# Two tokens to a partition in w's first loads, u spread by a product, W_out rows four to a partition

## The chip, the cores and the metric

The kernel runs on one core of one Trainium2 chip. The metric is the device time in microseconds, the median over several runs. A core has TensorE (PE, the matrix unit), VectorE (DVE), ScalarE (ACT), GpSimd (POOL) and SyncE (SP, which here only issues DMAs). All share an on-chip memory of 128 partitions; PE writes into PSUM.

## The reference

Two parts follow each other: a recurrent attention with a decay (B=4, H=8, S=768, D=48), and a two-layer MLP with a leaky ReLU on its 3072 output tokens (384 to 2048 to 384). All inputs and the output are float32.

```python
for t in range(S):
    kt, vt, rt, wt = k[:, :, t], v[:, :, t], r[:, :, t], w[:, :, t]
    cur = np.einsum('bhd,bhe->bhde', u[None] * kt, vt)
    y[:, :, t] = np.einsum('bhd,bhde->bhe', rt, state + cur)
    state = wt[:, :, :, None] * state + np.einsum('bhd,bhe->bhde', kt, vt)
x = y.transpose(0, 2, 1, 3).reshape(B * S, H * D)
h = x @ w_in
out = np.maximum(0.01 * h, h) @ w_out
```

## The kernel before, in words

**Attention.** The 3072 tokens are cut into 24 chunks of 128, six to a batch. A chunk has its 128 tokens on the partitions. Its w, r, k and v come in four loads (`load_in`, L190) of 192 KB, each 1024 runs of 192 bytes: one run per token and head. The steps of chunk i are named in the code, and the prediction uses these names:

- `log` (`a_log`, L229, ACT): the logarithm of w, as `lw`.
- `cum` (`a_cum`, L234 and L236, PE): the running sum of `lw` over the tokens, as a product with a triangle `tri`, and four one-column products with `ones` that give the chunk's whole sums for the decay of the state.
- `neg`: the negative sum that includes the token itself. In the first four chunks (`EARLY`) it is a second product with a triangle `trin` (`a_cum2`, L243, PE), later a DVE operation (`a_neg`, L247).
- `exp` and `exn` (L254, L257, ACT): exponentials of both sums. `kr` (L261, DVE): they are multiplied onto k and r.
- `trans` and `rkT` (L293, PE, then a copy L298 on ACT or L300 on DVE): the transpose of `kr`, eight blocks through the tile `trp`; for the later chunks (`BY_DMA`) one transposing DMA instead (L304, issued by SP).
- `scores` (L314, tile `at`), `m0` and `m1` (L322, DVE: the causal mask), `mix` (L333, L339, tile `y`), `ysb` (L347, DVE: adds the term of u).
- The term of u: `t1` (L265, r times `ukb`, POOL), `t2` (L269, times k, POOL), `diag` (L280, sum over D, DVE), `vsc` (L284, times v, POOL). `ukb` is u on all 128 partitions, loaded by SP (L193).
- The state: `kv` (L352, PE), `tt` (L360, or a copy), `st` (L370, POOL).
- `ytr` and `xT` (L380, PE, then a copy L388 on ACT): y transposed into `xT`, which the MLP reads; for the last chunks (`Y_BY_DMA`) a transposing DMA (L383).

**MLP.** W_in and W_out come in four quarters of 768 KB each (L200, L207) into float32 buffers, and DVE casts each to bfloat16 (L214, L217). The tokens are taken in blocks of 128 or 256 (`sizes`). For a block, `hid` (L409, tile `hp`) makes the 2048 hidden values in 16 groups of 128 columns of W_in, three matmuls for each; `act` (L415, ACT) applies the leaky ReLU into `gt`; `out` (L421, tile `op`) makes 128 tokens of output with 16 matmuls, in four parts that each need one quarter of W_out; `copy` (L428) and `issue` (L432) on ACT store them.

**Order.** The order of all instructions is written by the kernel itself before it emits anything. The class `Order` holds every step with its engine, a cost, the steps that it needs and the PSUM buffers it takes. It picks again and again the step that can begin earliest by these costs, and the instructions are emitted in that order, so each engine's list is fixed. Steps of rank 100 and above (the MLP) fill PE between those of the attention. Loads go out in the order of the list `queue`, all on SP's queue:

```python
queue = [('in', 0), ('u', 0), ('in', 1), ('in', 2), ('w_in', 0), ('in', 3), ('w_in', 1), ('w_in', 2), ('w_in', 3), ('in', 4), ('w_out', 0), ('w_out', 1), ('w_out', 2), ('w_out', 3)] + [("in", i) for i in range(5, NCH)]
```

Ahead of PE's first steps, up to a planned time of `WARM`, gaps are filled with dummy products of 512 columns (`scratch`, L548). The constants `tri`, `trin` and the identity are made on POOL, `ones`, the operand of the dummies and the zeroed padding on DVE. PSUM's eight buffers are given out as one for `cum`, one for `trp`, three for the rest of the attention (`att`) and three for the MLP (`mlp`, which also serves `neg` of the first chunks).

Of the kernel before, what the change touches and what calls it, by code (L numbers as in the profile page):

```python
# [8 lines left out]
F32 = mybir.dt.float32  # L9
# [6 lines left out]
class Order:  # L16
# [20 lines left out]
    def run(self, pools):  # L37
# [3 lines left out]
        taken = {p: [] for p in pools}  # L41
# [9 lines left out]
        def ready(name):  # L51
            t = 0.0
            for n in self.steps[name][6]:
                n = self.real(n)
                if n not in ends:
                    return None
                same = self.steps[n][0] == self.steps[name][0] != "DMA"
                t = max(t, ends[n] - (self.steps[n][4] if same else 0.0))
            want = {}
            for pool, _ in self.steps[name][7]:  # L60
                want[pool] = want.get(pool, 0) + 1
            for pool, n in want.items():
                old = len(taken[pool]) + n - 1 - pools[pool]
                for x in range(max(0, old - n + 1), old + 1):
                    until = self.real(taken[pool][x])
                    if until not in ends:
                        return None
                    t = max(t, ends[until])
            return t

        while any(todo.values()):
# [23 lines left out]
            ends[item[2]] = t + took + lag  # L95
            for pool, until in takes:
                taken[pool].append((until, item[2][1]) if isinstance(until, str) else until)
# [7 lines left out]
def kernel(  # L105
# [11 lines left out]
    nc = tc.nc  # L117
# [18 lines left out]
    inpool = ctx.enter_context(tc.tile_pool(name="inpool", bufs=NIN))  # L136
    work = ctx.enter_context(tc.tile_pool(name="work", bufs=3))
    gpool = ctx.enter_context(tc.tile_pool(name="gpool", bufs=2))
    opool = ctx.enter_context(tc.tile_pool(name="opool", bufs=NOUTB))
    ps_cum = ctx.enter_context(tc.tile_pool(name="ps_cum", bufs=1, space=bass.MemoryType.PSUM))  # L140
    ps_tr = ctx.enter_context(tc.tile_pool(name="ps_tr", bufs=1, space=bass.MemoryType.PSUM))
    ps_att = ctx.enter_context(tc.tile_pool(name="ps_att", bufs=3, space=bass.MemoryType.PSUM))
# [3 lines left out]
    trin = const.tile([128, 128], BF16, name="trin")  # L146
# [4 lines left out]
    lw_b = [const.tile([128, H, 64], BF16, name=f"lw{i}") for i in range(NB3)]  # L151
    kr_b = [const.tile([128, 2 * H, 64], BF16, name=f"kr{i}") for i in range(NB3)]
# [6 lines left out]
    def constants():  # L159
        nc.gpsimd.memset(tri[:], 1.0)  # L160
# [4 lines left out]
        nc.gpsimd.memset(trin[:], -1.0)  # L165
        nc.gpsimd.affine_select(
            out=trin[:], in_=trin[:], compare_op=ALU.is_ge, fill=0.0, base=0,
            pattern=[[1, 128]], channel_multiplier=-1,
        )
# [3 lines left out]
        for t in lw_b + kr_b:  # L173
            nc.vector.memset(t[:, :, D:64], 0.0)
# [7 lines left out]
    def load_in(i, name):  # L182
        b, c = divmod(i, C)
        src = {"w": w, "r": r, "k": k, "v": v}[name]
        if not ins[i]:
# [6 lines left out]
    def load_u():  # L192
        nc.sync.dma_start(out=ukb[:], in_=u.rearrange("h d -> (h d)").partition_broadcast(128))  # L193
# [11 lines left out]
    def load_w_out(q):  # L205
# [3 lines left out]
            in_=moe_w_out[q * JQ * 128 : (q + 1) * JQ * 128, :].rearrange("(t p) n -> p t n", p=128),  # L209
# [20 lines left out]

    def a_cum(i):
        lw = lw_b[i % NB3]
        cum = att[i]["cum"] = ps_cum.tile([128, 512], F32, name="cum")
# [7 lines left out]
    def a_cum2(i):  # L241
        cum2 = att[i]["neg"] = ps_mlp.tile([128, H, D], F32, name="cum2", tag="mlp")
        nc.tensor.matmul(cum2[:], lhsT=trin[:], rhs=lw_b[i % NB3][:, :, 0:D], start=True, stop=True)  # L243
# [45 lines left out]
    def a_trans(i):  # L289
        trp = att[i]["trp"] = ps_tr.tile([128, 2, NP, 128], BF16, name="trp", tag="tr")  # L290
# [102 lines left out]
    sizes = [256, 256, 128, 128, 128, 128, 128, 128, 128, 128, 128, 128, 128, 128, 128, 256, 128, 256, 256]  # L393
# [7 lines left out]
    def m_hid(q, j, nj):  # L401
# [4 lines left out]
        for jj in range(nj):  # L406
            wq, f0 = divmod((j + jj) * 128, FQ)
            for t in range(KT):
                nc.tensor.matmul(  # L409
                    hp[:, jj, :], lhsT=w_in_b[:, wq, t, f0 : f0 + 128],  # L410
# [28 lines left out]
    BY_DMA = range(11, NCH)  # L439
    Y_BY_DMA = range(14, NCH)  # L440
    WARM = 18.0
    RCAST = -1
    SLACK = 1.2
    RACT = 12
# [3 lines left out]
    add("const", "POOL", 2.2, constants, rank=-1)  # L448
    users = []
    users = []  # L450
    users = []
    queue = [('in', 0), ('u', 0), ('in', 1), ('in', 2), ('w_in', 0), ('in', 3), ('w_in', 1), ('w_in', 2), ('w_in', 3), ('in', 4), ('w_out', 0), ('w_out', 1), ('w_out', 2), ('w_out', 3)] + [("in", i) for i in range(5, NCH)]
    for kind, n in queue:
        if kind == "u":
            add("u", "DMA", 0.55, load_u, lag=1.95)
            continue
        past_user = users[-NIN:][:1] if len(users) >= NIN else []
        if kind == "in":
            for x in ("w", "r", "k", "v"):
                add((x, n), "DMA", 1.07, load_in, n, x, lag=1.95, needs=past_user)  # L460
            users.append(("done", n))
        else:
            load, cast = (load_w_in, cast_w_in) if kind == "w_in" else (load_w_out, cast_w_out)
            add((kind, n), "DMA", 2.3, load, n, lag=1.95, needs=past_user)
            add(("cast", kind, n), "DVE", 0.97, cast, n, needs=[(kind, n)], rank=RCAST)
            users.append(("cast", kind, n))
    for i in range(NCH):
        c = i % C

        def step(name, eng, took, f, *needs, args=(), lag=0.06, takes=()):  # L470
            add((name, i), eng, took, f, i, *args, lag=lag, rank=-1 if eng == "DMA" else i, takes=takes,
# [6 lines left out]
        step("log", "ACT", 0.52, a_log, "w", *past(3, "cum"))  # L478
        step("cum", "PE", 0.27, a_cum, "log", *past(1, "exp", "neg"), lag=0.18)
        step("exp", "ACT", 0.49, a_exp, "cum", *past(3, "st", "kr"))  # L480
        if early:
            step("neg", "PE", 0.17, a_cum2, "log", "cum", lag=0.18, takes=(("mlp", "exn"),))
# [4 lines left out]
        step("t1", "POOL", 1.0, a_t1, "r", ("u",), *past(2, "t2"))  # L487
# [4 lines left out]
        if i in BY_DMA:  # L492
            step("rkT", "DMA", 1.6, a_rkT_dma, "kr", *past(3, "mix"), lag=2.2)
            order.alias(("trans", i), ("rkT", i))
        else:
            step("trans", "PE", 0.45, a_trans, "kr", *past(1, "rkT"), lag=0.3)
# [85 lines left out]
```

## Time and profile before

| | |
|---|---|
| median of 7 runs | 190.17 us (188.21 to 191.35) |
| the profiled execution | 188.21 us, with a span of 186.5 us |
| PE busy | 176.3 us, 95% of the span, 2138 matmuls |
| DVE, ACT, POOL busy | 113.6, 110.4 and 114.5 us |
| hid (L409) | 912 matmuls: 672 of 128 columns, 240 of 256 |
| out (L421) | 384 matmuls of 384 columns |
| DMA | 34.8 MB in 125063 packets, 187 GB/s in the mean |
| granted PE clock | 0.999 |

How to read the rows. In the page, a row of 40 digits cuts the span into 40 slices; each digit is the busy share in tenths. A row of a stage has, after its two ends, for PE, weight loads (PEld), DVE, ACT and POOL the busy microseconds and the number of instructions, and then the granted clock, the mean share of the 16 DMA engines and GB/s. A row of the timeline has the start in microseconds, the length, the engine ("SPq" is SP's queue of issued DMAs), the line, what is written and read, a count, and in brackets how long the engine stood idle before it and what released it. A row of a group has line, engine, operation, tiles and shapes with a count, then the busy time, the mean in ns, and the idle time before with what ended it. The recorded length of one matmul includes the way through the array, so matmuls overlap: their pace is read from the time that a series takes.

### The profile page before, as it was taken

What the parts mean: (1) busy time and instruction counts of PE and PEld (TensorE: products, weight loads), DVE (VectorE), ACT (ScalarE), POOL (GpSimd) and SP (SyncE); (2) the same over time, 40 slices, a digit from 0 to 9 for tenths busy, and PEclk for the clock granted to TensorE, in tenths of its full rate; (3) what the DMA queues carried; (4) which work ended last, traced back from release to release, by engine and by line L of the source; (5) the groups of instructions that cost most, each with busy time, mean ns of one, the idle gap of its engine ahead of it and who ended that gap; (6) DMA issues with size and microseconds to landing.
All of it is one profiled execution on the core that took longest, in us unless ns stands there. A gap on an engine that the chain in (4) does not pass through costs nothing.

```text
span 186.5 us, 5284 instructions
## 1 busy us (share of the span) xinstructions
PE 176.3 (95%) x2138; PEld 132.3 (71%) x2140; DVE 113.6 (61%) x184; ACT 110.4 (59%) x216; POOL 114.5 (61%) x142
## 2 busy tenths in 40 slices
PE   7999659899999999999999999999999999999993
PEld 2555547766777978797788788778867886787751
DVE  2277895584588799995796677453776574550000
ACT  3465747832756875684785576467456874364721
POOL 3299675604848999999788876653868488320000
PEclk9999999999999999999999999999999999999999
DMA  6999899799999989999899999699989999712012
GB/s 117 206 188 272 191 385 204 268 374 206 224 241 185 219 156 210 175 233 184 189 211 185 165 213 199 121 227 171 222 176 218 158 200 162 192 25 63 0 42 84
DMA packets 125063, 34.80 MB, mean 187 GB/s; under 512 B 118256, under 2 KB 123504, under 8 KB 125040
## 3 DMA queue, kind: packets, MB, share of 16 engines
q1 hardware_dynamic: 121584, 29.76, 84.3%
q10 hardware_dynamic: 3456, 4.72, 8.2%
q8 instruction: 16, 0.26, 0.6%
q14 instruction: 7, 0.06, 0.1%
HBM read 25.36 MB, written 4.72 MB: 161 GB/s over the span
## 4 chain that ended last, share of the span: by engine, by line
PE 68%; SPq 13%; DMA 13%; ACT 2%; issue 1%; POOL 1%; ACTq 0%; POOLq 0%
PE op L421 28%; PE hp L409 27%; SPq L190 11%; DMA in<-in_w_dram 9%; DMA in<-in_k_dram 4%; PE at L314 3%; PE cum L234 2%; PE y L339 2%; PE trp L293 1%; SPq L200 1%; PE y L333 1%; PE kv L352 1%; PE ytr L380 1%; ACT lw L229 1%; ACT osb L428 1%
## 5 line engine op out<-in xcount | busy, mean ns | idle before, releaser
L409 PE MATMUL hp<-xT,w_in_b 128*128 128x128 bf16 (+1 forms) x912 | 71.3, 233 | 1.0 <-DVE w_in_b L214 1.0
L421 PE MATMUL op<-w_out_b,gt 128*128 128x384 bf16 x384 | 69.6, 326 | 0.0
L409 PEld LDWEIGHTS <-w_in_b 128*128 128x128 bf16 x912 | 61.5, 98 | 6.8 <-DVE w_in_b L214 1.6
L415 ACT ACTIVATE gt<-hp 128x512 bf16<-128x512 f32 x96 | 55.3, 597 | 14.0 <-PE hp L409 11.2
L421 PEld LDWEIGHTS <-gt 128*128 128x128 bf16 x384 | 34.9, 98 | 20.2
L322 DVE TENSOR_TENSOR mt<-at,tri 128x512 bf16<-128x512 f32 x48 | 30.9, 682 | 12.0 <-PE at L314 9.1
L370 POOL TENSOR_TENSOR st<-tt,e 48x192 bf16<-48x192 f32 x40 | 25.2, 630 | 19.6 <-DVE tt L360 16.7
L261 DVE TENSOR_TENSOR kr<-e,in 128x768 bf16<-128x768 f32 x24 | 27.9, 1164 | 11.7 <-ACT e L257 6.2
L269 POOL TENSOR_TENSOR t<-t,in 128x384 f32<-128x384 f32 x24 | 28.7, 1194 | 9.2 <-DMA in<-in_k_dram 8.1
L265 POOL TENSOR_TENSOR t<-in,ukb 128x384 f32<-128x384 f32 x24 | 26.2, 1093 | 11.9 <-DMA in<-in_r_dram 5.9
L284 POOL TENSOR_TENSOR vsc<-in,diag 128x384 f32<-128x384 f32 x24 | 21.8, 909 | 8.1 <-DVE diag L280 5.7
L428 ACT COPY osb<-op 128x384 f32<-128x384 f32 x24 | 11.4, 477 | 23.5 <-PE op L421 23.4
L229 ACT ACTIVATE lw<-in 128x384 bf16<-128x384 f32 x24 | 12.5, 522 | 13.3 <-DMA in<-in_w_dram 12.9
L247 DVE SCALAR_TENSOR_TENSOR neg<-cum,lw 128x384 f32<-128x384 f32 x20 | 11.0, 551 | 14.0 <-ACT e L254 14.0
L347 DVE TENSOR_TENSOR ysb<-y,vsc 128x384 bf16<-128x384 f32 x24 | 13.3, 553 | 8.1 <-PE y L339 6.8
L254 ACT ACTIVATE e<-cum 128x388 f32<-128x388 f32 x24 | 11.9, 495 | 10.3 <-PE cum L236 3.7
L280 DVE TENSOR_REDUCE diag<-t 128x8 f32<-128x384 f32 x24 | 13.1, 544 | 3.7 <-POOL t L269 3.7
L548 PE MATMUL scratch<-idle 128*128 128x512 bf16 x44 | 13.0, 430 | 1.4 <-DVE idle L172 1.3
L257 ACT ACTIVATE e<-neg 128x384 f32<-128x384 f32 x20 | 10.5, 524 | 5.7 <-DVE neg L247 5.1
L276 POOL CAST vb<-in 128x384 bf16<-128x384 f32 x20 | 13.0, 649 | 0.9 <-DMA in<-in_v_dram 0.8
L314 PE MATMUL at<-rkT 48*128 48x128 bf16 x192 | 9.5, 219 | 1.9 <-ACT rkT L298 1.9
L314 PEld LDWEIGHTS <-rkT 48*128 48x128 bf16 x192 | 5.4, 94 | 6.1 <-ACT rkT L298 3.1
(43 smaller groups left out, 129.8 us busy)
## 6 DMA issues: line engine op xcount, KB each, us to landing
in<-in_w_dram SPq DMA_DIRECT2D x24, 192.0 KB, 4.6
in<-in_r_dram SPq DMA_DIRECT2D x24, 192.0 KB, 4.5
in<-in_k_dram SPq DMA_DIRECT2D x24, 192.0 KB, 4.7
in<-in_v_dram SPq DMA_DIRECT2D x24, 192.0 KB, 4.5
out_dram<-osb ACTq DMA_DIRECT2D x24, 192.0 KB, 3.5
ws<-in_moe_w_in_dram SPq DMA_DIRECT2D x4, 768.0 KB, 6.7
ws<-in_moe_w_out_dram SPq DMA_DIRECT2D x4, 768.0 KB, 7.3
rkT<-kr SPq DMA_TRANSPOSE x13, 4.3
```

The source lines that it names most:

```text
L190: nc.sync.dma_start(out=ins[i][name], in_=src[b, :, c * L : (c + 1) * L, :].rearrange("h p d -> p h d"))
L229: nc.scalar.activation(out=lw_b[i % NB3][:, :, 0:D], in_=ins[i]["w"], func=AF.Ln)
L261: nc.vector.tensor_tensor(out=kr_b[i % NB3][:, :, 0:D], in0=e, in1=ins[i]["kr"], op=ALU.mult)
L265: nc.gpsimd.tensor_tensor(out=t1[:], in0=flat(ins[i]["r"]), in1=ukb[:], op=ALU.mult)
L269: nc.gpsimd.tensor_tensor(out=flat(t2[:]), in0=att[i]["t1"][:], in1=flat(ins[i]["k"]), op=ALU.mult)
L284: nc.gpsimd.tensor_tensor(out=vsc[:], in0=ins[i]["v"], in1=att[i]["diag"][:].unsqueeze(2).to_broadcast([128, H, D]), op=ALU.mult,)
L314: nc.tensor.matmul(ats[x][:, p, :], lhsT=rkT[r0 : r0 + D, 0, p, :], rhs=rkT[r0 : r0 + D, 1, p, :], start=True, stop=True,)
L322: nc.vector.tensor_tensor(out=att[i]["mt"][:, x], in0=att[i]["ats"][x][:], in1=tri[:].unsqueeze(1).to_broadcast([128, NP, 128]), op=ALU.mult,)
L370: nc.gpsimd.tensor_tensor(out=sn[r0 : r0 + D, :, x * D : (x + 1) * D], in0=tt[r0 : r0 + D, :, x * D : (x + 1) * D], in1=el[r0 : r0 + D, :] ...
L409: nc.tensor.matmul(hp[:, jj, :], lhsT=w_in_b[:, wq, t, f0 : f0 + 128], rhs=xT[:, t, t0 : t0 + mb], start=(t == 0), stop=(t == KT - 1),)
L415: nc.scalar.activation(out=gts[q][:, j : j + nj, :], in_=hps.pop((q, j))[:], func=AF.Prelu, alpha=0.01)
L421: nc.tensor.matmul(ops[q, ts][:], lhsT=gts[q][:, j, ts * 128 : (ts + 1) * 128], rhs=w_out_b[:, j, :], start=(j == 0), stop=(j == NFT - 1),)
```

## The change

- The w of two neighbouring chunks (0 and 1, 2 and 3) is loaded by one DMA, `load_wp`: partition p holds tokens 2p and 2p+1 of the 256, a run of 384 bytes for each head. `a_logp` takes the logarithm of both chunks at once. Chunk 2m then lies on partitions 0 to 63 and chunk 2m+1 on 64 to 127, so `a_cum` and `a_cum2` of these chunks make each sum by two products over 64 partitions, for even and odd tokens, with triangles `tri2` and `trin2` that fit this order. The one buffer for w pairs makes the second load wait for the first logarithm.
- u is loaded as one row of 1536 bytes, issued by ACT; a product with a row of ones (`spread_u`, float32) puts it on 128 partitions in PSUM, and DVE copies it to `ukb`.
- A quarter of W_out is loaded with four neighbouring rows on each partition. So that `gt` fits, `m_hid` takes W_in's columns four apart.
- The `Order` gives PSUM buffers to whichever is free instead of in turn, `cum` and `trp` share one pool of five with `att`, several costs and ranks (`OFF`, `RCAST`, `RACT`) are others, `sizes` has nine blocks of 256 tokens where there were five, chunk 10's `rkT` is now made by DMA, and the y of chunks 14 to 17 is transposed on PE instead of by DMA. Before the first 6 us of plan a dummy is counted at 0.45 us.

```diff
     def load_u():
-        nc.sync.dma_start(out=ukb[:], in_=u.rearrange("h d -> (h d)").partition_broadcast(128))
+        nc.scalar.dma_start(out=u_row[:], in_=u.rearrange("h d -> (h d)").rearrange("(a n) -> a n", a=1))
+
+    def spread_u():
+        ub = stage["u"] = ps_att.tile([128, DM], F32, name="ub", tag="att")
+        nc.tensor.matmul(ub[:], lhsT=one_row[:], rhs=u_row[:], start=True, stop=True)
+
+    def copy_u():
+        nc.vector.tensor_copy(out=ukb[:], in_=stage["u"][:])
+
+    def load_wp(m):
+        t = ins[2 * m]["wp"] = wpool.tile([128, H, 2 * D], F32, name="wp")
+        b, c = divmod(2 * m, C)
+        nc.sync.dma_start(
+            out=t[:], in_=w[b, :, c * L : (c + 2) * L, :].rearrange("h (p j) d -> p h (j d)", j=2)
+        )
...
-            in_=moe_w_out[q * JQ * 128 : (q + 1) * JQ * 128, :].rearrange("(t p) n -> p t n", p=128),
+            in_=moe_w_out[q * JQ * 128 : (q + 1) * JQ * 128, :].rearrange("(p t) n -> p t n", p=128),
...
+    def a_logp(m):
+        t = ins[2 * m]["wp"]
+        nc.scalar.activation(
+            out=lwp_b[m][:, :, :, 0:D].rearrange("p j h d -> p h j d"),
+            in_=t.rearrange("p h (j d) -> p h j d", j=2), func=AF.Ln,
+        )
+
     def a_cum(i):
+        if i < EARLY:
+            r0, m = 64 * (i % 2), i // 2
+            cum = att[i]["cum"] = ps_att.tile([128, 512], F32, name="cum", tag="att")
+            for j in range(2):
+                nc.tensor.matmul(
+                    cum[:, 0:DM], lhsT=tri2[r0 : r0 + 64, j, 2 * r0 : 2 * r0 + 128],
+                    rhs=lwp_b[m][r0 : r0 + 64, j, :, 0:D], start=(j == 0), stop=False, skip_group_check=True,
+                )
+            for p in range(NP):
+                for j in range(2):
+                    nc.tensor.matmul(
+                        cum[:, DM + p : DM + p + 1], lhsT=pair(lwp_b[m][r0 : r0 + 64, j], p),
+                        rhs=ones[r0 : r0 + 64, :], start=False, stop=(p == NP - 1 and j == 1),
+                        skip_group_check=True,
+                    )
+            return
...
-        nc.tensor.matmul(cum2[:], lhsT=trin[:], rhs=lw_b[i % NB3][:, :, 0:D], start=True, stop=True)
+        r0, m = 64 * (i % 2), i // 2
+        for j in range(2):
+            nc.tensor.matmul(
+                cum2[:], lhsT=trin2[r0 : r0 + 64, j, 2 * r0 : 2 * r0 + 128],
+                rhs=lwp_b[m][r0 : r0 + 64, j, :, 0:D], start=(j == 0), stop=(j == 1),
+            )
...
-    sizes = [256, 256, 128, 128, 128, 128, 128, 128, 128, 128, 128, 128, 128, 128, 128, 256, 128, 256, 256]
+    sizes = [256, 256, 128, 128, 128, 128, 256, 256, 256, 128, 256, 128, 256, 256, 256]
...
-            wq, f0 = divmod((j + jj) * 128, FQ)
+            wq, f0 = divmod(j + jj, JQ)
             for t in range(KT):
                 nc.tensor.matmul(
-                    hp[:, jj, :], lhsT=w_in_b[:, wq, t, f0 : f0 + 128],
+                    hp[:, jj, :], lhsT=w_in_b[:, wq, t, f0::JQ],
                     rhs=xT[:, t, t0 : t0 + mb], start=(t == 0), stop=(t == KT - 1),
                 )
...
-    BY_DMA = range(11, NCH)
-    Y_BY_DMA = range(14, NCH)
+    BY_DMA = range(10, NCH)
+    Y_BY_DMA = range(18, NCH)
     WARM = 18.0
-    RCAST = -1
+    OFF = {'exn': -1.5, 'log': -1.5, 'trans': -2.5, 'ytr': -0.5, 'exp': -2.5, 'scores': -0.5, 't2': 1.5, 't1': -2.5, 'ysb': 1.5, 'vb': 1.5, 'vsc': 1.5}
+    RCAST = 5
     SLACK = 1.2
-    RACT = 12
+    RACT = 0
...
-    steps = order.run({"att": 3, "mlp": 3})
+    steps = order.run({"att": 5, "mlp": 3})
```

What this does to the lists of the engines, read from the built programs: SP issues three loads fewer ahead of the second quarter of W_in (u and two of w); PE's list loses 23 of its 46 dummies (three then stand ahead of u's product, and two between it and chunk 0's sums), eight transposes and 192 hid matmuls, and gains 12 y transposes; in PE's new order 60 hid matmuls of 256 columns stand in one row behind chunk 4's sum, and chunk 4's transposes and scores come after the first `out` matmuls.

## The prediction

> **What bounds the kernel now.** I read the busy rows by slice first, then the mean by stage, then the timeline of the first 40 us, and last what the vector engine does there. The first two say where TensorE (PE) is not full:
>
> ```profile
> PE   7999659899999999999999999999999999999993
> ...
> DMA  6999899799999989999899999699989999712012
> ```
> ```profile
> 5.00:20.00 15.00, 13.57 (x136) 7.61 (x137) 8.66 (x13) 8.82 (x16) 10.81 (x12) 1.00 1.12 210
> 20.00:39.00 19.00, 15.16 (x175) 12.36 (x176) 13.85 (x21) 13.62 (x27) 11.31 (x12) 1.00 1.01 284
> 39.00:60.00 21.00, 20.75 (x248) 15.01 (x245) 14.46 (x23) 10.04 (x22) 11.59 (x14) 1.00 1.05 238
> 60.00:184.00 124.00, 123.08 (x1579) 95.94 (x1577) 75.21 (x120) 76.10 (x151) 79.22 (x95) 1.00 0.90 165
> ```
>
> From 39 us to the end PE is busy to within 1.2 us of 145. Before 20 us its busy time is mostly the 44 dummy products; from 20 to 39 us it idles 3.8 us. DMA is full throughout. So time can be gained by having real products start earlier, or by shortening PE's own list; anything hidden behind PE after 39 us is worth nothing. The timeline shows the head's milestones (start, length, then what):
>
> ```profile
> 3.68 1.07 SPq L193 DMA_DIRECT2D ukb<-in_u_dram  x1
> ...
> 6.53 0.96 DVE L261 TENSOR_TENSOR kr<-e,in 128x768 bf16<-128x768 f32 x1 [4.24 <-ACT e L257]
> ...
> 21.13 1.47 PE L409 MATMUL hp<-xT,w_in_b 128*128 128x256 bf16 x12
> ```
> ```profile
> 29.59 0.95 DVE L214 CAST w_in_b<-ws 128x1536 bf16<-128x1536 f32 x1
> ...
> 31.76 4.09 PE L409 MATMUL hp<-xT,w_in_b 128*128 128x256 bf16 x36
> ...
> 39.19 2.77 PE L421 MATMUL op<-w_out_b,gt 128*128 128x384 bf16 x16
> ```
>
> Real MLP work begins at 21.13; the last quarter of W_in is cast at 30.54; the first W_out product starts at 39.19, the milestone I use. Counting every matmul of PE's list at its pace (12 of 128 columns take 0.67 us, 48 of 256 take 5.24: about N x 0.417 ns + 2.7), the list from there to the last product (183.29) is 141.5 us long; it took 144.1, so 2.6 us is stall.
>
> **The loads.** By landing times in the trace a load of 1024 packets of 192 B takes 1.05 us of the queue, W_in's quarters (2048 B rows) 2.05 to 2.15, W_out's (1536 B) 2.11, u 1.04 (its 128 packets take 106 ns each, against 65 for other packets of that size).
> - Removed: u, 1.04, and w of chunks 1 and 3, 2.10.
> - Each w pair is still 1024 packets, of 384 B, a size that before does not show. Packets of 192, 256, 1536 and 2048 B take 15, 18, 65 and 84 ns, a line of 8 ns + 37 ns per KB: 22 ns. 64 per engine make 1.4 us, 0.35 more than one load; ends 1.05 (as 192 B) and 2.1 (no gain), and I take 1.4.
> - W_out in 6144 B rows: by the line 237 ns, 8 per engine, 1.9 us, 0.2 less each; ends 0 and 0.3.
>
> So chunk 0 comes 0.35 later, chunk 1 1.7 earlier, W_in's last three quarters and chunk 4 2.4 earlier (1.04+2.10-0.70), and all after W_out 3.2. The second pair's load waits on SP until the first pair's Ln is done (near 5.1 us); SP issued its eighth load at 5.89, so nothing queues behind that.
>
> **u.** It goes to ACT's queue behind the table load (0.80 to 2.08), then a one-row fp32 product, then a DVE copy (0.55, the ysb row; DVE idles 4.24 us before its first kr). The product stands in PE's list ahead of all cumulative sums. No fp32 product is in the trace. Loads landed some 2 us beyond their transfer, so u lands at 3 us if issued beside the table load and near 4.5 if after it; the product is then 0.2 us (bf16 pace) to 1.3[...]. The first sum could start at 5.2 anyway: the delay is 0 to 1.4. I take 0, the early issue. In exchange POOL's 5.6 us wait for u goes, which released nothing needed early. The larger masks on POOL (eight instructions instead of six, four of them on 512 columns at some 0.5 us, against 0.2 to 0.3 on 128) end near 4.4 us, inside that old wait.
>
> *Clock.* In before nine dummies from 1.29 take 0.43 us each, and after 5.6 us 0.22. "TensorE: Matmul & The Clock Gate", Part 1 of the Trainium skill, asks for about 3.4 us of sustained work before full rate. After the change only three dummies precede u's product and two follow. By the rule a hole while waiting for u keeps the first sums at half rate, about 0.7 us on chunk 0; by the row, if u is early, nothing. I charge nothing here and carry it in the second case.
>
> **The sums of chunks 0 to 3.** K is 64 now: two products for one (0.16 more), eight one-column products for four (0.11), two for one in the second sum (0.16). 0.27 of it lies ahead of chunk 0's exp. The joint Ln is 768 wide: 0.85 by the slope of the 384 and 512 rows (0.52, 0.60), 0.33 more. Chunk 0's kr moves from 6.53 to about 7.3 (0.35 load + 0.33 + 0.27, less 0.2 that the old sum waited behind a dummy).
>
> **What is late next: DVE.** Here the loads' 2.4 us are not all kept. DVE's groups from 6 to 31 us:
>
> ```profile
> L322 DVE TENSOR_TENSOR mt<-at,tri 128x512 bf16<-128x512 f32 x8 | 5.2, 681 | 3.5 <-POOL t L269 2.6 <-PE at L314 0.9
> L261 DVE TENSOR_TENSOR kr<-e,in 128x768 bf16<-128x768 f32 x4 | 4.8, 1197 | 4.2 <-ACT e L257 4.2
> L214 DVE CAST w_in_b<-ws 128x1536 bf16<-128x1536 f32 x4 | 4.2, 1056 | 1.2 <-DMA ws<-in_moe_w_in_dram 1.2
> L280 DVE TENSOR_REDUCE diag<-t 128x8 f32<-128x384 f32 x4 | 2.2, 547 | 0.4 <-POOL t L269 0.4
> L347 DVE TENSOR_TENSOR ysb<-y,vsc 128x384 bf16<-128x384 f32 x4 | 2.2, 546 | 0.0
> L360 DVE TENSOR_TENSOR tt<-kv,st 128x384 f32<-128x384 f32 x3 | 1.6, 542 | 0.0
> ```
>
> That is 20.2 us between the first kr (6.53) and the last W_in cast (30.54), 24.0 us: 3.8 of idling. The changed list has the same instructions there, so it cannot end before 7.3 + 20.2 = 27.5. Waits remain, 0.55 until chunk 1's k lands (8.75 to 9.3) and 1.1 until chunk 2's second exp, which stands behind ytr, the sums and two exps, so the cast ends near 29.2, 1.3 earlier. In the new PE order 60 products of 256 columns then stand unbroken (6.55 us), where before chunk 4's sum, transposes and scores and their waits lay between: the first W_out product comes at 35.8, 3.4 earlier. W_out's first quarter is there (lands 34.2, cast by 35.3). The PE list from that product on is 142.1 us, 0.6 longer, since chunk 4's steps moved behind it: **net 2.8 us**.
>
> **The rest of the plan.** Twelve more ytr products (0.67 us) against eight fewer transposes (0.45), and 192 products of 256 columns for 384 of 128 (0.5 saved), are in that 142.1. Four y transposes leave SP's queue and one rkT joins it: their loads were hidden, and go to ACT as xT copies (4 x 0.48, ACT 59% busy). Freely shared PSUM removes some waits. Against that the new order stands tighter: in six of 18 chunks only 0.8 to 1.0 us of other PE work lies between y and ytr, where y's end and its sum on DVE (0.2+0.17+0.56) need about that; in before it was two of 14. I charge 0.4 for it. Larger blocks in the middle need two chunks of xT at once; the list keeps 0.8 to 5 us of other work behind the last ytr. **Sum: -2.4 us**, so the profiled execution goes from 188.21 (span 186.5) to 185.8. That execution was the fastest of seven; the median lay at 190.17, so I forecast 187.8.
>
> **A rule against the change: strided weights.** W_out's new rows force W_in's columns to be taken four apart, so 720 weight loads read every fourth bf16; before has none such. Row: a 128-column hid product follows the last after 56 ns, weights included. The same page (LDWEIGHTS) gives columns/1.2 ns without fast weight load, 107 ns, which the row shows is not what happens; its section on weight-path modes says fast load reads 32 bits at once, which a stride of four would half waste, yet also allows a column step to 1,024. If the fast load were lost, the 288 products of 128 columns would pay 51 ns each (14.7 us) and the 432 of 256 columns, 109 ns long, nothing. "SBUF — State Buffer" (Door 1, cachelines) calls two hits per 16 B line free, which a step of 8 B meets. Ends 0 and 14.7; I take 0, nearest to the 56 ns row. No run shows it yet.
>
> **Cases.** Over 1% (1.9 us) is about what a measurement of this kernel tells from no change.
> - *Forecast, 0.54*: 187.8, own range 186.4 to 189.0.
> - *u's product or the wide packets eat the head, 0.21*: u late and PE cold put kr at 9 us; DVE, then dense, passes 1.4 to 2 of it on: 189.4. The same result if pairs cost 2.1. For: the table load ahead on ACT. Against: DVE idle after its first kr.
> - *Steady stalls shrink too, 0.12*: of 2.6 us, 1.5 to 2 go with DMA lighter by 3 us and PSUM shared: 186.0. For: many Ln start the moment w lands. Against: PE hides most of that.
> - *Strided weights, 0.13*: slower. Half-rate fast loads (estimate 65 ns) cost 288 x 9 = 2.6 us and merely cancel the gain; the full price gives 187.8 + 14.7 = 202.5. It decides from about 8 ns per 128-column product; most of this chance is at 191 to 193.
>
> Faster by over 1% (under 188.3): 0.54 x 0.8 + 0.12 + a little of the second, 0.57. Within: the rest of both, 0.28. Slower: 0.15. The range reaches from the third case to the cheap end of the fourth.
>
> **What would show it.** Right: w_in_b's last cast ends at 28.5 to 30, the first W_out product starts at 35 to 37, 12 hid products of 128 columns still take 0.67 us, and W_out quarters land 1.9 us apart. Wrong: those 12 take more than 0.75; the first kr starts after 8.5; or PE idles over 2 us between 60 and 184.

## The result, and the profile after

| kernel | median | range | runs |
|---|---|---|---|
| before | 189.95 us | 187.85 to 192.93 | 64 |
| changed | 188.67 us | 186.29 to 190.17 | 27 |

The ratio is 0.989, with a 95% interval of 0.9866 to 0.9914: the change makes the kernel 1.1% faster. This ratio and those below leave out executions more than 1.5% above the fastest of their kernel, while medians and counts are of all. The forecast was 187.8 with a range of 185.3 to 191.2.

The executions of the changed kernel fall into two groups. In 15 of its first 28 (the profiled one included) PE's mean granted clock was 0.996 or more, and their median is 187.0 us. In the other 13 it was about 0.99, and their median is 189.3. The profile taken first is of the second kind (189.77 us, span 188.0). Its busy rows by slice (PEclk is the granted clock, in tenths):

```profile
PE   7999869999999999999999999999999999999992
PEclk9999978999999999999999999999999999999998
DMA  6999799999999999979978998799998889522102
```

PE's row of before had a 6 and a 5 in its fifth and sixth slice. Here a 6 stands in the sixth (23.5 to 28.2 us), and the clock row dips there and in the next. DMA stays full up to its last six slices. A profile of the other kind was taken in the first series of runs (187.38 us, span 185.7). It is the first run of the experiments, after_again. Its stages, cut as before's were (PE, PEld, DVE, ACT, POOL, then clock, DMA share, GB/s):

```profile
5.00:20.00 15.00, 14.04 (x139) 7.63 (x139) 9.35 (x14) 9.39 (x17) 10.80 (x13) 1.00 1.31 222
20.00:39.00 19.00, 16.58 (x185) 14.73 (x186) 14.38 (x21) 13.53 (x26) 11.35 (x12) 1.00 1.00 327
39.00:60.00 21.00, 20.80 (x272) 15.78 (x271) 15.88 (x25) 11.73 (x24) 12.28 (x16) 1.00 1.07 211
60.00:184.00 124.00, 121.68 (x1360) 95.45 (x1357) 72.42 (x116) 76.68 (x152) 73.56 (x93) 1.00 0.80 159
```

The clock column takes off only stretches that the trace records at half rate; the time before PE's first full rate is not one of them, so 1.00 stands even in the first row. From 20 to 39 us PE is idle for 2.4 us instead of 3.8. In the last row 1.85 of the 2.32 idle microseconds lie after the last product, which now ends at 182.15. The head's milestones in the timeline of the same execution:

```profile
0.83 0.53 ACTq L204 DMA_DIRECT2D u_row<-in_u_dram  x1
...
2.68 1.64 PE L208 MATMUL ub<-u_row,one_row 1*128 1x384 f32 x2
...
4.76 0.84 ACT L258 ACTIVATE lwp<-wp 128x768 bf16<-128x768 f32 x1 [2.68 <-DMA wp<-in_w_dram]
...
7.86 0.96 DVE L314 TENSOR_TENSOR kr<-e,in 128x768 bf16<-128x768 f32 x1 [2.95 <-ACT e L310]
...
29.12 1.08 DVE L239 CAST w_in_b<-ws 128x1536 bf16<-128x1536 f32 x1
...
30.32 6.72 PE L462 MATMUL hp<-xT,w_in_b 128*128 128x256 bf16 x60
...
36.88 0.81 PE L474 MATMUL op<-w_out_b,gt 128*128 128x384 bf16 x4
```

The first kr starts 1.3 us later than before, and the first W_out product 2.3 us earlier (36.88 against 39.19). The head therefore gained 2.3 us of the 3.4 that were meant, though it began late.

In the execution with the dip the same series of 12 products, and the two steps after it, read:

```profile
26.72 2.75 PE L462 MATMUL hp<-xT,w_in_b 128*128 128x256 bf16 x12
...
32.35 6.74 PE L462 MATMUL hp<-xT,w_in_b 128*128 128x256 bf16 x60
...
38.93 0.81 PE L474 MATMUL op<-w_out_b,gt 128*128 128x384 bf16 x4
```

Twelve products of 256 columns take 1.50 us in the other execution, 2.75 here. The granted clock was one half from 26.29 to 29.70 us. The first W_out product comes 2.05 later: 0.67 of it was there already before this stretch (these 12 products begin at 26.72 against 26.05, and chunk 2's kr at 17.42 against 16.75), and the half-rate stretch adds the rest.

### The profile page after: what moved, and what is told of

Same layout as the page of the kernel before. It is cut to its first block, busy times and chain, and to the rows that moved or that the text cites. A ratio compares the mean times of both kernels' runs of the same rounds, so it can differ in the third digit from the quotient of the medians.

```text
span 188.0 us, 4892 instructions
## 1 busy us (share of the span) xinstructions
PE 179.2 (95%) x1954; PEld 135.3 (72%) x1955; DVE 114.8 (61%) x187; ACT 113.0 (60%) x218; POOL 111.0 (59%) x144
## 4 chain that ended last, share of the span: by engine, by line
PE 75%; DVE 7%; DMA 5%; POOL 4%; ACT 3%; issue 3%; ACTq 1%; POOLq 0%; DVEq 0%
PE hp L462 30%; PE op L474 29%; PE at L367 3%; DMA rkT<-kr 3%; DVE kr L314 3%; DVE mt L375 2%; PE scratch L609 2%; DMA wp<-in_w_dram 2%; PE trp L346 2%; PE y L392 2%; POOL t L322 2%; PE y L386 2%; PE cum L282 1%; PE ytr L433 1%; ACT osb L481 1%
## 5 line engine op out<-in xcount | busy, mean ns | idle before, releaser
L462 PE MATMUL hp<-xT,w_in_b 128*128 128x256 bf16 (+1 forms) x720 | 73.3, 254 | 0.3 <-ACT xT L441 0.2
L468 ACT ACTIVATE gt<-hp 128x512 bf16<-128x512 f32 x96 | 57.0, 597 | 23.8 <-PE hp L462 20.0
L462 PEld LDWEIGHTS <-w_in_b 128*128 128x128 bf16 x720 | 63.2, 114 | 4.4 <-DVE w_in_b L239 0.7
L375 DVE TENSOR_TENSOR mt<-at,tri 128x512 bf16<-128x512 f32 x48 | 30.8, 684 | 11.7 <-PE at L367 11.5
L318 POOL TENSOR_TENSOR t<-in,ukb 128x384 f32<-128x384 f32 x24 | 25.2, 1049 | 14.9 <-DMA in<-in_r_dram 14.5
L423 POOL TENSOR_TENSOR st<-tt,e 48x192 bf16<-48x192 f32 x40 | 22.5, 562 | 19.1 <-DVE tt L413 13.0
L337 POOL TENSOR_TENSOR vsc<-in,diag 128x384 f32<-128x384 f32 x24 | 22.7, 946 | 14.7 <-DVE diag L333 14.3
L322 POOL TENSOR_TENSOR t<-t,in 128x384 f32<-128x384 f32 x24 | 26.5, 1106 | 1.4
L481 ACT COPY osb<-op 128x384 f32<-128x384 f32 x24 | 11.5, 477 | 14.7 <-PE op L474 14.4
L254 ACT ACTIVATE lw<-in 128x384 bf16<-128x384 f32 x20 | 10.4, 520 | 3.5 <-DMA in<-in_w_dram 3.5
L413 DVE TENSOR_TENSOR tt<-kv,st 128x384 f32<-128x384 f32 x16 | 8.8, 549 | 2.3 <-issue 1.5
L609 PE MATMUL scratch<-idle 128*128 128x512 bf16 x22 | 8.7, 536 | 1.3 <-DVE idle L180 1.3
## 6 DMA issues: line engine op xcount, KB each, us to landing
in<-in_r_dram SPq DMA_DIRECT2D x24, 192.0 KB, 4.7
in<-in_k_dram SPq DMA_DIRECT2D x24, 192.0 KB, 4.7
in<-in_v_dram SPq DMA_DIRECT2D x24, 192.0 KB, 4.7
out_dram<-osb ACTq DMA_DIRECT2D x24, 192.0 KB, 3.2
in<-in_w_dram SPq DMA_DIRECT2D x20, 192.0 KB, 4.7
```

The source lines that it names most:

```text
L318: nc.gpsimd.tensor_tensor(out=t1[:], in0=flat(ins[i]["r"]), in1=ukb[:], op=ALU.mult)
L322: nc.gpsimd.tensor_tensor(out=flat(t2[:]), in0=att[i]["t1"][:], in1=flat(ins[i]["k"]), op=ALU.mult)
L337: nc.gpsimd.tensor_tensor(out=vsc[:], in0=ins[i]["v"], in1=att[i]["diag"][:].unsqueeze(2).to_broadcast([128, H, D]), op=ALU.mult,)
L375: nc.vector.tensor_tensor(out=att[i]["mt"][:, x], in0=att[i]["ats"][x][:], in1=tri[:].unsqueeze(1).to_broadcast([128, NP, 128]), op=ALU.mult,)
L423: nc.gpsimd.tensor_tensor(out=sn[r0 : r0 + D, :, x * D : (x + 1) * D], in0=tt[r0 : r0 + D, :, x * D : (x + 1) * D], in1=el[r0 : r0 + D, :] ...
L462: nc.tensor.matmul(hp[:, jj, :], lhsT=w_in_b[:, wq, t, f0::JQ], rhs=xT[:, t, t0 : t0 + mb], start=(t == 0), stop=(t == KT - 1),)
```

## The experiments

Each ratio is to runs of the kernel before on the same chip. The medians of before there are 190.92 us (after_again to a_w), 189.72 (a_none to a_warm2) and 190.49 (the last four), so medians of different series cannot be compared to half a per cent.

| run | what it is | median us | ratio, 95% |
|---|---|---|---|
| after_again | the changed kernel | 187.48 | 0.9926 (0.9874 to 0.9979) |
| a_rows | W_out rows as before | 188.29 | 0.9944 (0.9906 to 0.9983) |
| a_u | u loaded as before | 188.44 | 0.9950 (0.9901 to 0.9998) |
| a_w | w loaded chunk by chunk | 188.27 | 0.9930 (0.9881 to 0.9979) |
| a_none | new order, all loads as before | 189.66 | 1.0022 (0.9993 to 1.0052) |
| a_plan | new loads, old order | 189.79 | 1.0011 (0.9979 to 1.0043) |
| a_warm | changed, dummies to 32 us | 187.41 | 0.9871 (0.9818 to 0.9924) |
| a_warm2 | a_warm, u's product later | 187.78 | 0.9910 (0.9873 to 0.9947) |
| a_warm_again | a_warm | 187.81 | 0.9894 (0.9847 to 0.9941) |
| a_warm_w | a_warm, w chunk by chunk | 188.07 | 0.9888 (0.9848 to 0.9927) |
| a_warm_rows | a_warm, W_out rows as before | 188.03 | 0.9894 (0.9847 to 0.9941) |
| b_warm | before, dummies to 32 us | 190.82 | 1.0018 (0.9984 to 1.0051) |

### Undoing one part at a time

The unchanged kernel ran again beside three that each take back one part. a_rows:

```diff
-            in_=moe_w_out[...].rearrange("(p t) n -> p t n", p=128),
+            in_=moe_w_out[...].rearrange("(t p) n -> p t n", p=128),
...
-                    hp[:, jj, :], lhsT=w_in_b[:, wq, t, f0::JQ],
+                    hp[:, jj, :], lhsT=w_in_b[:, wq, t, f0 : f0 + 128],
```

a_u loads u by SP to all partitions, behind chunk 0's v, and has no product and no copy for it:

```diff
+        if i == 0 and name == "v":
+            nc.sync.dma_start(out=ukb[:], in_=u.rearrange("h d -> (h d)").partition_broadcast(128))
```

a_w loads each chunk's w by itself and makes its sums over 128 partitions:

```diff
+        for x in range(2):
+            b, c = divmod(2 * m + x, C)
+            nc.sync.dma_start(out=t[:, x], in_=w[b, :, c * L : (c + 1) * L, :].rearrange("h p d -> p h d"))
```

> The changed kernel again. In its first profile TensorE's granted clock was at full rate only from 12.6 us and fell to half from 26.3 to 29.7 us, where the kernel before was at full rate from 5.3 us on. Theory (the change gains some 2 us in the head, and a half-rate window in the head takes about as much back in some executions): runs fall into two groups, near 187 with a mean clock of 0.997 or more, and near 189.3 with 0.991 or less; ratio to before 0.985 to 0.992. Rival (the two groups have nothing to do with the clock): clock and time don't go together.

> The changed kernel with W_out's rows and W_in's columns as before (512 runs of 1536 B to a quarter, weights read side by side); the order of all engines is the same. Theory (strided weights free, wide rows worth 0.2 us of the queue each): W_out's quarters land 2.1 apart instead of 1.93, the time is that of the changed kernel within 0.4 us, since the first W_out product waits for the hidden products and not for these loads. Rival (strided weight reads cost, up to 9 ns on each of 288 products): 0.5 to 2.6 us faster than the changed kernel.

> The changed kernel with u as before: one load of 128 rows by SP behind chunk 0's v; no product, no copy; the order of the other steps is the same. Theory (u's 1.04 us of the queue matter): all loads behind chunk 0 land about 1 us later, and the first product of W_out comes 0.3 to 0.8 us later; the time is 0.3 to 0.8 us above the changed kernel. Rival (the product gates chunk 0 and keeps TensorE cold): chunk 0's sums start no later, TensorE is at full rate sooner, and the time is the same or up to 1 us lower.

> The changed kernel with one token to a partition in the first four chunks: each pair load is two loads of 192 B runs at the same place in the order, two logarithms, one product for each sum. Theory (a pair costs 1.6 us of the queue where two loads cost 2.1): loads behind the first pair land 0.5 us later, behind the second 1 us later, but chunk 0's sums start about 0.8 us sooner (its own w lands at 3.9, log 0.52); the time is within 0.6 us of the changed kernel. Rival (the packets are what the change gains by): slower by 1 us or more.

The two groups came as expected in after_again (nine executions at 0.997 or more with a median of 187.4, three at 0.989 or less with 189.2). No single part is shown to make the gain. The three medians lie 0.8 to 1.0 us above the unchanged kernel's, more than each theory had allowed, but the intervals of the four ratios overlap. The three differences add up to 2.6 us, no less than the 1.8 us or so that taking back all the loads costs below (by the ratios of a_none and after_again), so the parts are not shown to be worth nothing either. Only a_rows settles its question, since it can be read from the pace. In stretches of twelve or more after 32 us, hid products of 128 columns follow each other after 56.35 ns with columns taken four apart (after_again), 55.95 with neighbouring ones (a_rows), and 55.93 in before. Of 256 columns it is 110.12 against 109.52. So the step of four costs about 0.4 ns x 288 + 0.6 ns x 432 = 0.4 us in all. The recorded length of a weight load did grow. The changed kernel's page has 114 ns for the strided loads, beside 98 for those of `gt`, which are not strided:

```profile
L462 PEld LDWEIGHTS <-w_in_b 128*128 128x128 bf16 x720 | 63.2, 114 | 4.4 <-DVE w_in_b L239 0.7
...
L474 PEld LDWEIGHTS <-gt 128*128 128x128 bf16 x384 | 35.7, 98 | 20.0
```

So 16 ns more in the record of a load that overlaps the products were at most 0.6 ns of pace. In a_w the clock row matters: 11 of its 12 executions had a mean clock under 0.996, and the one that did not took 186.86 us.

### The order alone, the loads alone

I then supposed that the new order made most of the gain. a_none keeps the new order, blocks (four fewer than before, not six as its expectation says), ranks and PSUM sharing, with every load and sum as in before. a_plan keeps the new loads and takes the old lists:

```diff
-    sizes = [256, 256, 128, 128, 128, 128, 256, 256, 256, 128, 256, 128, 256, 256, 256]
+    sizes = [256, 256, 128, 128, 128, 128, 128, 128, 128, 128, 128, 128, 128, 128, 128, 256, 128, 256, 256]
...
-    OFF = {'exn': -1.5, ...}
-    RCAST = 5
+    OFF = {}
+    RCAST = -1
...
-    RACT = 0
+    RACT = 12
```

(`BY_DMA` and `Y_BY_DMA` too are those of before; the sharing of PSUM stays that of the changed kernel.)

> The changed kernel's order, blocks, ranks and PSUM sharing, with w, u and W_out loaded as before (one token to a partition, u by SP as 128 rows, one row of W_out to a partition). Theory (after single undoings that moved the time by half a microsecond or less, most of the gain is the new order: W_out's first product behind 60 unbroken hidden products, 6 blocks fewer): within 0.7 us of the changed kernel, so near 188. Rival (the three loads make the gain together): 189.5 or more, like the kernel before; the first W_out product after 38.5 us.

> The changed kernel's loads with the blocks, ranks and transposing DMAs of before (sizes, OFF, RCAST, RACT, BY_DMA, Y_BY_DMA). Theory (the order makes most of the gain): within 0.7 us of the kernel before, so 189.5 to 191. Rival (the loads make it): near 188.

The theory fell: the order alone gives 1.0022 and the loads alone 1.0011. **Neither half gives a gain that can be measured without the other**, and the two profiles show what each lacks. (a_none's has no drop of the clock, a_plan's has one.) With the old loads, the last W_in casts wait for their transfers, as DVE's timeline of a_none shows:

```profile
27.96 0.96 DVE L216 CAST w_in_b<-ws 128x1536 bf16<-128x1536 f32 x1 [0.28 <-DMA ws<-in_moe_w_in_dram]
...
30.09 0.96 DVE L216 CAST w_in_b<-ws 128x1536 bf16<-128x1536 f32 x1 [0.24 <-DMA ws<-in_moe_w_in_dram]
```

The last quarter lands at 30.07, where in the changed kernel it lands at 28.03. The twelve products that need it first start at 31.11, behind the cast, the others follow, and the first W_out product stands at 38.38, 1.5 later than in after_again. With the old order and the new loads the casts are done at 29.18, earlier than in any other kernel here. The profile of a_plan shows what then comes late on PE:

```profile
25.84 4.49 PE L462 MATMUL hp<-xT,w_in_b 128*128 128x256 bf16 x24 [0.59 <-DVE w_in_b L239]
...
33.75 2.12 PE L462 MATMUL hp<-xT,w_in_b 128*128 128x256 bf16 x18 [1.05 <-ACT xT L441]
...
39.88 1.30 PE L474 MATMUL op<-w_out_b,gt 128*128 128x384 bf16 x7
```

In the old order 24 hid products stand ahead of chunk 3's y on PE. DVE, with its casts done, waits 1.63 us for that y, so `ysb` starts at 30.81 (28.66 in after_again), and xT, which ACT makes behind other work, ends at 33.70 instead of 31.41. PE waits 1.05 us for it. The 60 products ahead of W_out, which take 6.72 us unbroken in the new order, are broken up by chunk 4's sum, transposes and scores and by this wait, and take from 30.71 to 39.9. This profile also has a half-rate stretch, 26.6 to 30.0 us, in which most of the 24 products fall: they take 4.49 us, where full rate would need about 2.8 (an estimate from 12 in 1.50 and 60 in 6.72). So 1.7 us of the lateness may be the clock's, and how much of the wait for xT would be left without it this profile cannot say. But 9 of a_plan's 14 executions had the full clock, and their median is still 189.5.

### The clock

The half-rate stretches begin and end on a grid of 3.41 us, and each drop in the profiles lasted one step of it. I divided each profile by its own grid. First the windows of the changed kernel as first profiled (columns as in a stage), and below them the emptiest window of after_again, whose grid lies otherwise:

```profile
19.46:22.87 3.41, 2.73 (x32) 2.00 (x30) 3.32 (x6) 2.70 (x5) 3.26 (x5) 1.00 0.77 208
22.87:26.28 3.41, 1.72 (x35) 1.30 (x34) 2.99 (x5) 2.07 (x5) 3.18 (x5) 1.00 0.98 326
26.29:29.70 3.41, 3.32 (x27) 2.32 (x24) 2.53 (x4) 1.21 (x3) 1.07 (x1) 0.50 1.15 324
```
```profile
21.45:24.86 3.41, 2.04 (x33) 1.71 (x30) 2.99 (x5) 2.37 (x4) 3.26 (x4) 1.00 1.04 368
```

PE is busy for 1.72 us of the window ahead of the drop. I then went through all windows of all fourteen profiles from the first full rate to 178 us. In six there is a drop, once each, and it follows the emptiest window of the profile: 1.5 us busy in a_w, 1.6 in a_warm_w and b_warm, 1.7 in the changed kernel and a_u, 1.85 in a_plan. In the eight without a drop the emptiest window has 1.87 (before), 2.0 (a_rows, after_again), 2.1 (a_none) and 2.67 or more (a_warm_rows, a_warm, a_warm2, a_warm_again). The window in question lies at 22 to 27 us in four of the six, but at 16 us in a_warm_w and at 99.5 us in b_warm. A stretch of 3.41 us that is slid freely over after_again finds one with only 1.53 us of work near 23 us, and in before one with 1.21. So the same program can drop or not by where the grid falls on its gaps. If that is so, filling these gaps must keep the clock. a_warm lets dummies stand in PE's planned gaps up to 32 us (37 instead of 23), each group into a PSUM buffer of its own so that it waits for no reader:

```diff
-    WARM = 18.0
+    WARM = 32.0
...
+                if at >= 16.0 and int((start - at) / 0.22) > 0:
+                    scratch = ps_mlp.tile([128, 512], F32, name="scratch", tag="mlp")
```

a_warm2 moves u's product behind chunk 1's sums as well, so that eight dummies stand ahead of the first sum:

```diff
-    add("ub", "PE", 1.2, spread_u, lag=0.2, rank=-3, needs=["u"], ...)
+    add("ub", "PE", 1.2, spread_u, lag=0.2, rank=1.5, needs=["u", ("neg", 1)], ...)
```

> The changed kernel with dummy products also in PE's planned gaps from 18 to 32 us (each group in a PSUM buffer of its own); nothing else changes. Theory (a half-rate window in the head costs the changed kernel about 1.8 us in a part of its executions, because PE does too little between 20 and 26 us): no execution with a mean clock under 0.996, the median at that of the undisturbed executions, near 187.4. Rival (the dummies delay real work or hold PSUM buffers): 188 or more.

> As with dummies to 32 us, and u's product moved behind chunk 1's sums, so that eight dummies run ahead of chunk 0's sums. Theory (the one-row float32 product and the few dummies keep PE at half rate until 11 to 13 us): full rate from 5.3 us on, chunk 0's first kr 0.5 to 0.8 us sooner (near 7.2 instead of 7.9), the time 0.2 to 0.8 us under the version with dummies alone. Rival (DVE is dense behind and ends at the same time): first kr sooner, the last cast of W_in and the time the same.

The stage of a_warm that was 16.58 us busy above:

```profile
20.00:39.00 19.00, 19.00 (x198) 15.77 (x199) 13.88 (x20) 13.61 (x26) 11.40 (x12) 1.00 1.01 308
```

None of a_warm's six executions had a clock under 0.996, against 16 of 40 of the changed kernel; two of a_warm2's eight had, at 0.99, and no profile shows where. a_warm2's eight dummies did not bring full rate earlier, against its theory: it began at 12.74 us, the first kr came at 7.52, and the time did not fall. Why not stayed open.

The last series repeats a_warm, takes the w pairs and the W_out rows back in it, and gives the dummies to the kernel before:

```diff
-    WARM = 18.0
+    WARM = 32.0
```

That is b_warm's edit, with the same lines for `scratch` as a_warm's; it has 65 dummies instead of 46. a_warm_w is a_warm with a_w's edit, a_warm_rows is a_warm with that of a_rows.

> The changed kernel with dummies in PE's planned gaps to 32 us, once more, beside the next three on one chip. Theory (dummies keep PE at full rate, and nothing else changes): no execution under 0.996, median 186.9 to 187.6, ratio to before 0.984 to 0.990.

> The same with one token to a partition in w's first four loads (two loads of 192 B runs in the place of a pair, sums of one product over 128 partitions). Theory (a pair saves 0.5 us of the queue and costs chunk 0 about 0.6 us, so the two cancel): within 0.4 us of the version with pairs. Rival (pairs do not pay): 0.4 us or more faster than it, and then the fastest of all.

> The same with pairs, but W_out's rows and W_in's columns as before. Theory (wide rows save 0.2 us of the queue for each quarter, strided weights cost 0.6 ns on each product of 256 columns, 0.3 us in all): within 0.4 us of the version with wide rows. Rival (quarters that land up to 1 us later hold the first W_out products): 0.5 us or more slower.

> The kernel before with dummies in PE's planned gaps to 32 us. Theory (the change's gain is its earlier hidden products, and the clock only decides how much of it an execution keeps): fewer executions under 0.996, but the median within 0.6 us of the kernel before. Rival (the gain of the best versions is the clock alone): 1 us or more faster than before, near 188.

a_warm held the clock again, in six of six. Its profile has the grid within 0.24 us of where the changed kernel's lay in the execution that dropped, and this window:

```profile
23.11:26.52 3.41, 3.40 (x44) 2.00 (x42) 3.08 (x5) 2.20 (x5) 3.18 (x5) 1.00 0.95 329
```

Chunk 2's kr is as late here as in that execution (17.47 and 17.42), but the first W_out product stands at 37.74, 1.19 earlier. So with the gap filled the drop goes, and 1.2 us of the head with it. The last product ends at 182.12, 2.4 earlier; the other 1.2 arises behind the first W_out product, where the versions of the changed kernel differ by up to 1.8 us (143.8 to 145.6 to the last product). The dummies add no speed beyond keeping the clock: a_warm's medians (187.41, 187.81) lie 0.4 above those of the changed kernel's executions without a drop (187.0, 187.4). Its ratios, 0.9871 and 0.9894, are among the lowest here, but their intervals take in 0.989, so it is not shown to beat the changed kernel.

b_warm raised the clock (19 of 22 executions at 0.996 or more, against 3 of 27 of before beside it) and not the speed: 1.0018. Drops are nothing that the change brought: 76 of the 91 executions of before in these series had a mean clock under 0.996. A half-rate step takes 3.41 x 0.5 / 188 = 0.009 off the mean (an estimate), so 0.99 is one step and 0.982 two. In each of the three series before's executions with two steps are slower than those with one, by 1.4 to 1.8 us (191.9 against 190.5, 191.4 against 189.6, 192.0 against 190.5). Since b_warm had no execution with two steps and was no faster, such drops look like the sign of a stall more than its cause. b_warm's profile, of the slowest of its 22 executions (193.53 us), shows one:

```profile
102.37 0.40 PE L314 MATMUL at<-rkT 48*128 48x128 bf16 x8 [1.79 <-DMA rkT<-kr]
```

DVE's last kr ahead of it was done at 99.3, but SP stood 3.24 us in the issue of a load of w and issued the transposing DMA only at 101.73; PE idled meanwhile, and the half-rate step of 102.95 to 106.36 followed. Whether such waits spread before's times in general is not shown. Nor is it excluded that the dummies cost b_warm something: in this profile its last cast ends at 32.16 and its first W_out product stands at 40.60.

Without w pairs (a_warm_w) or wide rows (a_warm_rows) the ratios are 0.9888 and 0.9894, the same within 0.5%. a_warm_w still dropped in three of six: its profile has a window of 1.64 us at 16.1 to 19.5, which the planned dummies do not cover. A gain of these parts one by one is below what the runs resolve; that loads as a whole are needed is what a_none shows.

## Why the prediction was right, step by step

The forecast held, with its own range (186.4 to 189.0) and its mechanism: earlier loads, 60 hid products in one row, and an earlier first W_out product. But less of the gain came than was said: 1.3 us of 2.4 on medians, and 0.8 between the profiles without a drop (2.1 by the ratio). The steps that failed all failed on the short side, and none made up for another; that 188.67 lies inside is owed to the width of the range. Milestones are of after_again, the profile without a drop.

- **The w pair: mis-sized.** A delay of 0.35 us was taken for the first load, with ends 0 and 1.05. It landed at 4.74 against 3.88, 0.86 later. The packets of the first pair took 22 ns, as the line gave, yet their engines were not full. The rows of the first 6 us, in slices of 0.15, of after_again and then of before:

```profile
DMA  0000000000000653479999999999999999999999
```
```profile
DMA  0000000000000388999999999999999999999999
```

  From 2.1 to 2.55 us the engines are three to five tenths busy in the first and eight to nine in the second. So the time per packet gave only a lower bound here. What held the engines back was not settled. The second pair took 1.58 us after the load before it, against 1.4, and its packets 32 ns.
- **Earlier loads: right in kind, too large.** Chunk 1's r, k and v landed 1.0 earlier than in before, where 1.7 was said, and W_in's last quarter at 28.03 instead of 29.53, 1.5 earlier, where 2.4 was said. W_out's first quarter came at 34.35 (34.2 said). The last W_in cast began 1.1 after its quarter had landed, so DVE and not the load set it.
- **Sums and the joint Ln: right.** From the landing of w to the first kr it was 2.65 us and is 3.12, 0.47 more, where the steps gave 0.40. The Ln took 0.84 (0.85 said). So of the 0.56 by which kr missed 7.3, the load is 0.51.
- **u: right, by room.** ACT issued it beside the table load, as chosen. The product took 1.64 us, above the upper end of 1.3, but ended at 4.32, ahead of the first sum. Nothing was late by it.
- **The clock: wrong.** Nothing was charged. By the trace's clock records full rate came at 5.26 us in before and at 11.2 and 12.6 in the changed kernel; with single w loads it came at 8.83 (a_w), with all old loads at 4.87 (a_none), and with u as before still at 12.96 (a_u). PE is not idle from 1.29 to 5.28: it runs dummies and the one-row product there, and still gets no full rate. Nor did the window from 5.81 to 9.22 us of the first profile bring it, which is filled without a hole, the greater part with sums over 64 rows. In a_w, whose sums are over 128 rows, a window with 3.19 us of work (5.41 to 8.83) did. So products over 64 rows seem to count for less; no run tests that alone. My second case had the late clock as u's doing and a kr at 9 us. What happened instead is, first, that chunk 2's kr goes with the time of full rate: among the profiles of the changed kernel, a_rows and the versions with dummies and pairs, it starts at 16.6 to 16.8 where full rate begins at 10.9 to 11.5, and at 17.2 to 17.5 where it begins at 12.6 to 12.9. And second, the rate can drop once near 26 us. "TensorE: Matmul & The Clock Gate", Part 1, of the Trainium skill speaks of a free-running window of about 3.4 us, which the grid of 3.41 agrees with, and of an idle window as what lowers the rate; here a window in which PE was half busy was enough. By that rule alone no drop was to be expected at 26 us. With and without a drop the medians differ by 1.8 us (the series of after_again) and 2.3 (the first 28).
- **DVE next: right in kind, 0.45 short.** DVE's groups from 6 to 31 us:

```profile
L375 DVE TENSOR_TENSOR mt<-at,tri 128x512 bf16<-128x512 f32 x8 | 5.1, 685 | 0.9 <-PE at L367 0.9
L314 DVE TENSOR_TENSOR kr<-e,in 128x768 bf16<-128x768 f32 x4 | 5.0, 1258 | 4.5 <-ACT e L310 3.7 <-DMA in<-in_k_dram 0.8
L239 DVE CAST w_in_b<-ws 128x1536 bf16<-128x1536 f32 x4 | 3.9, 984 | 0.0
```

  The 1.2 us wait of the casts for their transfers is gone: the last zero says so. Of kr's 4.5, 2.95 lie ahead of the first; what remains, 0.83 for chunk 1's k and 0.72 for an exp, is 1.55, near the 1.65 that was counted. The 0.9 for chunk 0's scores, and smaller waits for `t`, were not. With kr 0.56 late and 0.45 more of waits the last cast ends at 30.21 instead of 29.2, just outside the sign of 28.5 to 30 that was named. (The 20.2 us of the prediction adds recorded lengths that overlap: DVE was busy for 18.93 of before's 24.0 us, so the floor was nearer 26.2 than 27.5.)
- **60 hid unbroken: right.** 6.72 us for 6.55, starting 0.1 after the last cast. The first W_out product is 1.08 later than 35.8: 1.0 from the cast, the rest here.
- **The list after it: right.** From the first W_out product to the last it takes 145.3 us; 142.1 + 2.6 of stall + 0.4 for the tighter order gave 145.1. In a_rows and a_warm_again it was 144.3 and 144.4, so one execution is not a measure to 1 us. The third case (stalls shrink) did not show: from 60 us to the last product PE idles 0.5 us where before had 0.2. (The sign that I had named, over 2 us idle there, is met by 2.32 only because the work ends before 184.)
- **Strided weights: right.** 0.4 us, near the end of 0. W_out's four quarters land from 34.35 to 40.12, 1.92 apart, where 1.9 was said (2.22 in a_rows, from 34.63 to 41.30), and 12 products of 128 columns take 0.67.
- **The sum.** The steps gave -2.4 on the profiled execution (188.21 to 185.8); without a drop it was 187.38, a gain of 0.8. The last product ends 1.1 earlier, since the head gained 2.3 and not 3.4. On medians it is 1.3 with the drops and 2.9 for the executions without. The gain was thus read from a profile that does not stand for before's runs: at 188.21 it was among the fastest of 187.85 to 192.93, and its clock, 0.999, is rare (15 of 91 executions of before at 0.996 or more). The forecast put its gain on the median of seven instead, which was near the later median of 64 (190.17 and 189.95); that part was sound. What spreads before's runs stayed open.

## What to carry to other kernels

Loads that come earlier are worth what the lists behind them can take: ask which engine's order decides next, and try the two together. When one thins out filler work on TensorE, sum its busy time over the clock's own window (3.41 us here) at every place where the window can fall, and do not look at the longest idle hole alone. And judge such a change by the executions of each kind apart before a part of it is credited with half a per cent.

## What the runs showed of the hardware that was not expected

- A half-rate stretch on PE lasted 3.41 us each time, on a grid that lies differently in each execution. It followed windows with 1.85 us or less of recorded PE work and none with 1.87 or more, in fourteen profiles; matmul records can be missing and their ends are modelled, so the border is rough. What was seen is that half a window of work is near it.
- A one-row float32 product of 384 columns took 1.64 us before PE had its full rate, in two recorded instructions.
- The weights' step of four bf16 lengthened the recorded load by 16 ns (98 to 114) and the pace by 0.4 to 0.6 ns.
- A window of 3.41 us filled with work, the greater part over 64 rows, was not followed by full rate (5.81 to 9.22 us in the first profile); in b_warm 2.68 us of dummies over 128 rows were enough.
